# Channel attention and gated convolution: where the weight conversions and the norm sums of the first score pass run

## Chip, cores and metric

The kernel runs on one NeuronCore of a Trainium2 chip. The metric is the device time of one execution in microseconds (us); lower is better. A core has these engines, each with an instruction queue of its own that it works off in order: TensorE (PE, matmuls; PEld is its weight load), VectorE (DVE), ScalarE (ACT), GpSimd (POOL) and SyncE (SP), which here only issues DMAs. Operands lie in SBUF, 128 partitions wide, and matmul results in PSUM.

## The reference, cut to what matters

```
# q, k, v: (4, 6336, 256) float32; conv_w: (5, 256); w_val, w_out: (256, 256)
qn = q / (norm(q, axis=1) + 1e-6)            # norms over the 6336 rows, per channel
kn = k / (norm(k, axis=1) + 1e-6)
a  = softmax(kn^T @ qn / tau, axis=-1)       # 256 x 256 per batch
x  = v @ a
gate_pre[t] = sum over tap 0..4 of conv_w[tap] * x[t - 4 + tap]
out = (sigmoid(gate_pre) * (x @ w_val)) @ w_out
```

The three weights arrive as float64 and the rest as float32, so the kernel sees each weight as pairs of 32-bit integers and makes the float32 (or its high and low part) out of these itself.

## The kernel before, in words

**Two kinds of work.** For each of the four batches a *score pass* goes over all rows of q and k and gathers s = k^T q in one PSUM tile (`s_ps`) and the sums of the squares of q and k in two tiles (`acc`, named `acc_ps`, in PSUM, and `side`, named `acc`, in SBUF). A softmax makes the 256 x 256 weights from them. Then a *step* for each of 13 chunks of 508 rows takes v through two products, the five-tap gate, the sigmoid and the product with w_out. From the second batch on, the score pass of the next batch is mixed with the steps of this one. The first batch's score pass stands alone, at the head of the program: that is where the change is.

**The score pass in groups.** A batch's rows are cut into 17 groups. Group 0 holds one row per partition and a rest of 64 rows, groups 1 to 16 three rows per partition each. `load_group` fetches the q and the k of a group with two DMAs from the SP queue into one of six `raw` buffers, four groups ahead. `score_group` (L166) then puts out, per group:

- ScalarE: the squares `sq` of the group (L209), into one of two buffers. For a row that is *split*, also the high part `hi` (L192).
- VectorE: rows j < `nv` of `sq` are added to the sum in PSUM (L214).
- GpSimd: the other rows are added to the sum in SBUF (L214, too), and the low part of a split row is raw minus hi (L193).
- TensorE (L226): rows j < `nw` are multiplied as they are (*native*: two matmuls a row, which the trace records as four), the others as three products of their high and low parts (six matmuls a row).

In the first batch groups 0 to 10 have nw = 3 and nv = 2: all native, VectorE adds two rows and GpSimd one. Groups 11 to 16 have nw = 2 and nv = 3: two native rows and one split row, VectorE adds all three, GpSimd only makes the low part.

**What waits for what.** A group's squares need a free `sq` buffer, that is, the adds of an earlier group on both engines. The squares must be made before the `raw` buffer is loaded again. After group 16 the softmax begins: VectorE joins the sums into `acc_all` (L240), which waits for every add, ScalarE copies s out of PSUM (L242), and TensorE clears `s_ps` for the second batch (L231) behind that copy, does the second batch's group 0 and then sums `acc_all` over the partitions (L245). Five groups of the second batch, all native, fill TensorE while the softmax runs.

**The weights.** At group 6 the kernel asks for the weights. `prepare_weights(0)` (w_val and conv_w, into `wa`) is ten VectorE instructions and a reciprocal (L161), `prepare_weights(1)` (w_out, into `wb`, `wo_hi` and `wo_lo`) nine and a ScalarE copy, `wo_hi` (L149). L132, L136, L138, L140 and L144 read one tensor each; L134, L142, L146, L151 and L154 read two. All of these lie in SBUF. Both parts are generators, and from group 9 on each takes two instructions a group, so the two are mixed. A scheduler with a model of the times then sets the final order on each engine; `issue_after` and `behind(...)` hold it back.

## Time and profile before

| | |
|---|---|
| Median of 3 runs | 657.69 us (655.65 to 657.83) |
| The profiled execution | 655.7 us, of which 653.8 us are the span from the first to the last instruction |
| TensorE busy | 636.1 us, 97% of the span |
| VectorE, ScalarE, GpSimd busy | 521.7 us (80%), 465.7 us (71%), 362.1 us (55%) |

The profile's timeline gives, per engine, the start of an instruction in us from the span's start, how long it took, its line, its operation, what it writes and reads, how many alike were run together (x), and in brackets the idle time of the engine ahead of it with what ended it. An instruction that is held up inside the engine shows as a longer one. The chain of waits is followed back from the program's last instruction to what released each step.

### The profile page before, as it was taken

How to read it: one execution, taken by the hardware profiler on the slowest of the kernel's cores; microseconds unless marked ns; L12 is line 12 of the kernel's file. 1: busy time of each engine (PE TensorE's matmuls, PEld its weight loads, DVE VectorE, ACT ScalarE, POOL GpSimd, SP SyncE). 2: the span in 40 equal slices, each digit the busy share in tenths (PEclk: the TensorE clock that was granted, in tenths of full speed). 3: DMA queues.
4: the chain of work that ended last, by engine and by line, in shares of the span. 5: the costliest groups of instructions: out<-in, count | busy, mean ns of one | idle time of the engine just before them, and what ended most of it. 6: DMA issues, size and time to landing. Idle time of an engine off the chain costs nothing.

```text
span 653.8 us, 10657 instructions
## 1 busy us (share of the span) xinstructions
PE 636.1 (97%) x4008; PEld 570.3 (87%) x4008; DVE 521.7 (80%) x831; ACT 465.7 (71%) x607; POOL 362.1 (55%) x174
## 2 busy tenths in 40 slices
PE   7999999999999999999998999999999999999996
PEld 5878799998979999999997998999999798988886
DVE  3897689787878688778788688778778889888894
ACT  5465978867888768668688787777777755655564
POOL 2441896965837769659565497766763122312221
PEclk9999999999999999999999999999999999999999
DMA  8999875555635665545554375653222343443213
GB/s 272 336 320 335 267 233 154 152 170 162 188 99 175 186 195 176 167 136 173 177 178 127 113 222 168 179 182 103 65 80 76 113 126 102 114 129 105 65 51 99
DMA packets 107875, 105.75 MB, mean 162 GB/s; under 512 B 5744, under 2 KB 107312, under 8 KB 107824
## 3 DMA queue, kind: packets, MB, share of 16 engines
q1 hardware_dynamic: 82048, 79.76, 39.8%
q10 hardware_dynamic: 25776, 25.32, 13.7%
q8 instruction: 31, 0.51, 0.3%
q14 instruction: 20, 0.16, 0.1%
HBM read 79.11 MB, written 25.95 MB: 161 GB/s over the span
## 4 chain that ended last, share of the span: by engine, by line
PE 84%; DVE 4%; ACT 4%; DMA 3%; SPq 2%; POOL 1%; issue 1%; ACTq 0%; DVEq 0%
PE o_ps L404 21%; PE x_ps L345 19%; PE val_ps L345 19%; PE s_ps L226 17%; PE t_ps L335 6%; SPq L74 2%; DMA raw<-in_k_dram 1%; PE o_ps L294 1%; POOL hi L193 1%; DMA w_raw<-in_moe_conv_w_dram 1%; DMA v_raw<-in_v_dram 1%; ACT hi L192 1%; DVE acc_ps L214 1%; DVE gate L361 1%; DVE gate L374 1%
## 5 line engine op out<-in xcount | busy, mean ns | idle before, releaser
L361 DVE SCALAR_TENSOR_TENSOR gate<-x_ps,wa,gate 128x508 f32<-128x508 f32 (+1 forms) x416 | 275.4, 718 | 14.4 <-ACT gate L359 13.4
L193 POOL TENSOR_TENSOR hi<-raw,hi 128x1536 fp32r<-128x1536 f32 (+2 forms) x54 | 167.8, 3109 | 92.8 <-ACT hi L192 92.8
L388 POOL TENSOR_TENSOR g_lo<-gate,g_hi 128x1016 fp32r<-128x1016 f32 (+1 forms) x50 | 116.8, 2335 | 145.1 <-ACT g_hi L387 130.5
L214 DVE TENSOR_TENSOR acc_ps<-acc_ps,sq 128x512 f32<-128x512 f32 (+1 forms) x134 | 93.5, 698 | 73.9 <-ACT sq L209 70.7
L345 PE MATMUL x_ps<-v_hi,w 128*128 128x512 f32 (+1 forms) x416 | 138.1, 391 | 0.0
L345 PE MATMUL val_ps<-v_hi,w 128*128 128x508 f32 (+1 forms) x416 | 133.9, 384 | 0.8 <-ACT o_sb L414 0.7
L226 PE MATMUL s_ps<-hi 128*128 128x256 f32 (+1 forms) x852 | 121.0, 287 | 6.2 <-ACT hi L192 4.0
L226 PEld LDWEIGHTS s_ps<-hi 128*128 128x128 f32 (+1 forms) x852 | 110.7, 190 | 12.6 <-ACT hi L192 5.5
L404 PE MATMUL o_ps<-wo_hi,g_hi 128*128 128x256 f32 x400 | 113.3, 283 | 0.2 <-DVE gate L374 0.2
L414 ACT COPY o_sb<-o_ps 128x512 f32<-128x512 f32 x99 | 58.1, 588 | 76.1 <-PE o_ps L404 74.8
L404 PE MATMUL o_ps<-wo_lo,g_hi 128*128 128x256 f32 x400 | 112.2, 281 | 0.0
L404 PE MATMUL o_ps<-wo_hi,g_lo 128*128 128x256 f32 x400 | 111.8, 280 | 0.0
L209 ACT ACTIVATE sq<-raw 128x1536 f32<-128x1536 f32 (+3 forms) x69 | 96.0, 1393 | 16.3 <-DVE acc_ps L214 8.0
L214 POOL TENSOR_TENSOR acc<-acc,sq 128x512 f32<-128x512 f32 x58 | 76.3, 1315 | 38.9 <-ACT sq L209 38.5
L345 PEld LDWEIGHTS val_ps<-v_hi,w 128*128 128x128 f32 x416 | 77.2, 188 | 14.4 <-ACT o_sb L414 0.9
L345 PEld LDWEIGHTS x_ps<-v_hi,w 128*128 128x128 f32 x416 | 77.5, 188 | 13.9 <-DVE gate L361 0.2
L359 ACT ACTIVATE gate<-x_ps,wa 128x508 f32<-128x508 f32 (+1 forms) x104 | 68.1, 669 | 20.6 <-PE x_ps L345 20.3
L336 ACT CAST v_hi<-t_ps 128x512 fp32r<-128x512 f32 (+1 forms) x104 | 55.7, 568 | 35.7 <-PE t_ps L335 33.2
L345 PE MATMUL x_ps<-v_lo,w 128*128 128x512 f32 (+1 forms) x208 | 79.8, 384 | 0.0
L345 PE MATMUL val_ps<-v_lo,w 128*128 128x508 f32 (+1 forms) x208 | 79.3, 381 | 0.0
L374 DVE TENSOR_TENSOR gate<-val_ps,gate 128x508 f32<-128x508 f32 (+1 forms) x104 | 64.3, 657 | 17.1 <-ACT gate L367 14.4
L404 PEld LDWEIGHTS o_ps<-wo_hi,g_hi 128*128 128x128 f32 x400 | 75.3, 188 | 1.4 <-DVE gate L374 0.4
(84 smaller groups left out, 800.0 us busy)
## 6 DMA issues: line engine op xcount, KB each, us to landing
raw<-in_q_dram SPq DMA_DIRECT2D x64, 384.0 KB
raw<-in_k_dram SPq DMA_DIRECT2D x64, 384.0 KB
v_raw<-in_v_dram SPq DMA_DIRECT2D x44, 512.0 KB
out_dram<-o_sb ACTq DMA_DIRECT2D x47, 384.0 KB
out_dram<-o_sb ACTq DMA_DIRECT2D x47, 124.0 KB
v_raw<-in_v_dram SPq DMA_DIRECT2D x4, 384.0 KB
raw<-in_q_dram SPq DMA_DIRECT2D x4, 128.0 KB
raw<-in_k_dram SPq DMA_DIRECT2D x4, 128.0 KB
```

The lines of the kernel that those rows point to most:

```text
L193: nc.gpsimd.tensor_tensor(hi[r, js, :, 1, :], raw[r, js, :, :], hi[r, js, :, 0, :].bitcast(F32), ALU.subtract)
L209: nc.scalar.activation(sq[0:np_, ja:jb], raw[0:np_, ja:jb], AF.Square)
L214: eng.tensor_tensor(st[key][0:np_], st[key][0:np_], sq[0:np_, j], ALU.add)
L226: nc.tensor.matmul(st["s"][:, h, :], lhs, rhs, start=False, stop=stop and h == NH - 1 and n_ == len(ops) - 1)
L336: nc.scalar.copy(th[:, h, 0:w], tp[:, 0:w])
L345: marks["PRODUCT"] = nc.tensor.matmul(ps, wt[:, which, ws, ch, hs], vs[:, ch, lo:hi_], start=n_ == 0, stop=n_ == 3 * NH - 1)
L359: nc.scalar.activation(gate[:, h, 0:w], x_ps[:, 0:w], AF.Copy, scale=cw[:, h, 0:1])
L361: nc.vector.scalar_tensor_tensor(gate[:, h, 0:w], x_ps[:, tap:tap + w], cw[:, h, tap:tap + 1], gate[:, h, 0:w], ALU.mult, ALU.add)
L374: nc.vector.tensor_tensor(gate[:, h, 0:w], val_ps[:, 0:w], gate[:, h, 0:w], ALU.mult)
L388: nc.gpsimd.tensor_tensor(gl[:, :, 0:w], gate[:, :, 0:w], gh[:, :, 0:w].bitcast(F32), ALU.subtract)
L404: nc.tensor.matmul(o_ps[:, u * C:(u + 1) * C], gs[:, h, off:off + P], ws[:, h, :], start=n_ == 0, stop=n_ == 3 * NH - 1)
L414: marks["ACT"] = nc.scalar.copy(o_sb[:, j:j + len(pair), :], o_ps[:, 0:len(pair) * C].rearrange("p (j c) -> p j c", c=C))
```

## The change

Three things change in the first score pass and behind the first softmax:

- Groups 7 to 13 (`SIDE` = 7 to `MIXED` = 14) are all native, and VectorE adds only one of their three rows, GpSimd two. Before, groups 7 to 10 were native with one row for GpSimd, and 11 to 13 had a split row and no row for GpSimd. Groups 14 to 16 stay as they were.
- From group 7 on, three conversion instructions a group are put out, held behind the last VectorE add of that group, first all of `prepare_weights(0)`, then all of `prepare_weights(1)`.
- The ScalarE copy `wo_hi` leaves the generator and stands behind the first softmax, behind its last ScalarE instruction (L298).

```diff
-SIDE = 11
+SIDE, MIXED = 7, 14
...
-            if part:
-                nc.scalar.copy(wo_hi.rearrange("p h e -> p (h e)"), up.bitcast(F32))
...
-            nw, nv = (GROUP, 2) if g < SIDE else (2, 3)
+            nw, nv = (GROUP, 2 if g < SIDE else 1) if g < MIXED else (2, 3)
...
-            eng.tensor_tensor(st[key][0:np_], st[key][0:np_], sq[0:np_, j], ALU.add)
+            add = eng.tensor_tensor(st[key][0:np_], st[key][0:np_], sq[0:np_, j], ALU.add)
+            if key == "acc":
+                marks["DVE"] = add
...
-        if n >= 9:
-            for gen in prep:
-                for _ in range(2):
-                    next(gen, 0)
+        if n >= SIDE:
+
+            with behind("DVE"):
+                for _ in range(3):
+                    while prep and next(prep[0], 0) is not None:
+                        prep.pop(0)
...
     while stages:
         tick()
+    if WORDS == 2:
+        with behind("ACT"):
+            nc.scalar.copy(wo_hi.rearrange("p h e -> p (h e)"), w_raw[1][:, :, 1].bitcast(F32))
     for h in range(NH):
         transpose_v(*step(1), h)
```

In the changed kernel the lines of `prepare_weights` and `score_group` behind the removed two stand two lower: the adds are L212, the casts L190, the low parts L191, the last conversion of w_out L149.

**VectorE, the last conversions of w_out (`wb`, `w_raw_206`) and the end of the score pass.** Before, `sq_271` holds the squares of group 10, and `sq_290`, `sq_315`, `sq_356`, `sq_378`, `sq_397`, `sq_418` those of groups 11 to 16:

```order
L144 TENSOR_SCALAR w_raw_206<-w_raw_206 128x512
L151 SCALAR_TENSOR_TENSOR wo_lo_112<-w_raw_206,wb_110 128x512
L214 TENSOR_TENSOR acc_ps_120<-acc_ps_120,sq_271 128x512
L146 TENSOR_TENSOR w_raw_206<-w_raw_206,wb_110 128x512
L214 TENSOR_TENSOR acc_ps_120<-acc_ps_120,sq_271 128x512
L214 TENSOR_TENSOR acc_ps_120<-acc_ps_120,sq_290 128x512 x3
L214 TENSOR_TENSOR acc_ps_120<-acc_ps_120,sq_315 128x512 x3
L214 TENSOR_TENSOR acc_ps_120<-acc_ps_120,sq_356 128x512 x3
L214 TENSOR_TENSOR acc_ps_120<-acc_ps_120,sq_378 128x512 x3
```

Changed, `sq_294`, `sq_311`, `sq_344`, `sq_357`, `sq_375`, `sq_396` are groups 11 to 16:

```order
L212 TENSOR_TENSOR acc_ps_120<-acc_ps_120,sq_311 128x512
L142 SCALAR_TENSOR_TENSOR wb_110<-w_raw_206,wb_110 128x512
L144 TENSOR_SCALAR w_raw_206<-w_raw_206 128x512
L146 TENSOR_TENSOR w_raw_206<-w_raw_206,wb_110 128x512
L212 TENSOR_TENSOR acc_ps_120<-acc_ps_120,sq_344 128x512
L149 SCALAR_TENSOR_TENSOR wo_lo_112<-w_raw_206,wb_110 128x512
L212 TENSOR_TENSOR acc_ps_120<-acc_ps_120,sq_357 128x512 x3
L212 TENSOR_TENSOR acc_ps_120<-acc_ps_120,sq_375 128x512 x3
L212 TENSOR_TENSOR acc_ps_120<-acc_ps_120,sq_396 128x512 x3
L240 TENSOR_TENSOR acc_all_428<-acc_ps_120,acc_121 128x512
```

The last conversion stood between the adds of group 10, with 19 adds still to come; now it stands behind the add of group 13, with the nine adds of groups 14 to 16 to come. The first conversion (L132 of `wa`) now stands behind the add of group 7; before it stood between the two adds of group 6.

**GpSimd in the same stretch.** Before, from group 7 (`sq_225`) to group 16:

```order
L214 TENSOR_TENSOR acc_121<-acc_121,sq_225 128x512
L214 TENSOR_TENSOR acc_121<-acc_121,sq_239 128x512
L214 TENSOR_TENSOR acc_121<-acc_121,sq_253 128x512
L214 TENSOR_TENSOR acc_121<-acc_121,sq_271 128x512
L193 TENSOR_TENSOR hi_289<-raw_222,hi_289 128x2x256
L193 TENSOR_TENSOR hi_314<-raw_236,hi_314 128x2x256
L193 TENSOR_TENSOR hi_355<-raw_250,hi_355 128x2x256
L193 TENSOR_TENSOR hi_377<-raw_268,hi_377 128x2x256
L193 TENSOR_TENSOR hi_396<-raw_286,hi_396 128x2x256
L193 TENSOR_TENSOR hi_417<-raw_311,hi_417 128x2x256
```

Changed, again from group 7 (`sq_225`) to group 16 (`hi_395`):

```order
L212 TENSOR_TENSOR acc_121<-acc_121,sq_225 128x512 x2
L212 TENSOR_TENSOR acc_121<-acc_121,sq_242 128x512 x2
L212 TENSOR_TENSOR acc_121<-acc_121,sq_259 128x512 x2
L212 TENSOR_TENSOR acc_121<-acc_121,sq_276 128x512 x2
L212 TENSOR_TENSOR acc_121<-acc_121,sq_294 128x512 x2
L212 TENSOR_TENSOR acc_121<-acc_121,sq_311 128x512 x2
L191 TENSOR_TENSOR hi_356<-raw_273,hi_356 128x2x256
L212 TENSOR_TENSOR acc_121<-acc_121,sq_344 128x512
L191 TENSOR_TENSOR hi_374<-raw_291,hi_374 128x2x256
L212 TENSOR_TENSOR acc_121<-acc_121,sq_344 128x512
L191 TENSOR_TENSOR hi_395<-raw_308,hi_395 128x2x256
```

Ten instructions have become seventeen: four adds and six low parts before, fourteen adds and three low parts now, and all of the conversions stand beside them on VectorE.

**ScalarE behind the first softmax.** Before, the softmax's last cast (L298) is followed by the high part of the second batch's group 5 (`hi_611`):

```order
L289 COPY at_583<-o_ps_525 128x512
L359 ACTIVATE gate_558<-x_ps_559,wa_109 128x508
L359 ACTIVATE gate_558<-x_ps_571,wa_109 128x508
L298 CAST w_522<-o_ps_585 128x512
L192 CAST hi_611<-raw_460 128x6x256
L209 ACTIVATE sq_612<-raw_460 128x1536
```

Changed (that group's high part is `hi_590`):

```order
L289 COPY at_561<-o_ps_503 128x512
L359 ACTIVATE gate_536<-x_ps_537,wa_109 128x508
L359 ACTIVATE gate_536<-x_ps_549,wa_109 128x508
L298 CAST w_500<-o_ps_563 128x512
L525 CAST wo_hi_111<-w_raw_206 128x512
L190 CAST hi_590<-raw_438 128x6x256
L207 ACTIVATE sq_591<-raw_438 128x1536
```

The copy of w_out's high part, which stood between the squares of group 11 and the high part of group 12, now stands in front of that cast.

## Prediction

> **What bounds the kernel now.** I read the page first, then the chain of waits, then the timeline of each engine over the first 90 us, where the change is. The page:
>
> ```profile
> span 653.8 us, 10657 instructions
> PE 636.1 (97%) x4008; PEld 570.3 (87%) x4008; DVE 521.7 (80%) x831; ACT 465.7 (71%) x607; POOL 362.1 (55%) x174
> ```
>
> TensorE is busy for 97% of the span, so a change counts only where TensorE idles, or where it makes TensorE idle. TensorE's timeline of the first score pass and the start of the second:
>
> ```profile
> 4.25 34.65 PE L226 MATMUL s_ps<-raw 128*128 128x256 f32 x136 [1.85 <-DMA raw<-in_k_dram]
> 42.17 0.38 PE L226 MATMUL s_ps<-hi 128*128 128x256 f32 x1 [0.38 <-ACT hi L192]
> 43.54 0.86 PE L226 MATMUL s_ps<-hi 128*128 128x256 f32 x5 [0.98 <-POOL hi L193]
> 44.23 1.89 PE L226 MATMUL s_ps<-raw 128*128 128x256 f32 x8
> 46.67 1.89 PE L226 MATMUL s_ps<-raw 128*128 128x256 f32 x8
> 53.09 1.06 PE L226 MATMUL s_ps<-hi 128*128 128x256 f32 x6
> 54.83 0.50 PE L231 MATMUL s_ps<-zeros 128*128 128x512 f32 x1 [0.67 <-DMA v_raw<-in_v_dram]
> 57.18 0.70 PE L245 MATMUL o_ps<-acc_all,ones 128*128 128x256 f32 x2
> ```
>
> From 4.25 on it works without a gap through groups 0 to 10 and the two native rows of group 11. Then it waits for the high part (0.38 us at 42.17) and the low part (0.98 us at 43.54) of group 12. From 44.23 mixed groups follow each other every 2.44 us (46.67 - 44.23), and the pass ends at 54.15 (53.09 + 1.06). What held group 12 up is on ScalarE:
>
> ```profile
> 40.95 0.66 ACT L149 CAST wo_hi<-w_raw 128x512 fp32r<-128x512 f32 x1 [2.47 <-DVE w_raw L146]
> 52.96 0.63 ACT L209 ACTIVATE sq<-raw 64x512 f32<-64x512 f32 x1 [0.77 <-DVE acc_ps L214]
> 54.19 0.58 ACT L242 COPY s<-s_ps 128x512 f32<-128x512 f32 x1 [0.59 <-PE s_ps L226]
> ```
>
> The copy `wo_hi` stands idle for 2.47 us until VectorE has made its input, and the high part of group 12 is queued behind it. The other two rows are the end of the pass: the squares of the second batch's rest rows (52.96), which wait for VectorE's adds, then the copy of s (54.19), behind which TensorE clears `s_ps` (54.83) and, 2.35 us on, sums `acc_all` (57.18), which begins the softmax.
>
> Data is no bound there: the last k of the first batch is on the way from 38.96 to 47.78, in the chain of waits:
>
> ```profile
> 38.96 8.82 DMA raw<-in_k_dram
> ```
>
> **What the change removes.** The wait of ScalarE goes, and groups 11 to 13 need no high and low part. TensorE alone would then be the bound. A native group is a third of the 36 native matmuls at 61.62 (7.94 us, of which some 0.2 are the last one's tail), 2.59 us:
>
> ```profile
> 61.62 7.94 PE L226 MATMUL s_ps<-raw 128*128 128x256 f32 x36
> ```
>
> From 38.53 there are four records of group 11 (0.86), two native groups (5.18) and three mixed ones (7.32): 51.9, and with the last matmul's tail 52.1, against 54.15. That is the most the change can bring here: 2.0 us.
>
> **What it adds: a conflict of VectorE and GpSimd.** VectorE's rows while the conversions run, and GpSimd's in the same stretch:
>
> ```profile
> 25.39 0.70 DVE L142 SCALAR_TENSOR_TENSOR wa<-w_raw,wa 128x522 int32<-128x522 int32 x1
> 26.01 1.49 DVE L132 TENSOR_SCALAR wb<-w_raw 128x512 int32<-128x512 int32 x1
> 28.02 0.42 DVE L144 TENSOR_SCALAR w_raw<-w_raw 128x522 int32<-128x522 int32 x1
> 29.56 1.62 DVE L146 TENSOR_TENSOR w_raw<-w_raw,wa 128x522 int32<-128x522 int32 x1
> 32.05 0.68 DVE L214 TENSOR_TENSOR acc_ps<-acc_ps,sq 128x512 f32<-128x512 f32 x1
> 36.81 1.23 DVE L144 TENSOR_SCALAR w_raw<-w_raw 128x512 int32<-128x512 int32 x1
> 37.95 1.76 DVE L151 SCALAR_TENSOR_TENSOR wo_lo<-w_raw,wb 128x512 fp32r<-128x512 int32 x1
> ```
>
> ```profile
> 25.64 1.58 POOL L214 TENSOR_TENSOR acc<-acc,sq 128x512 f32<-128x512 f32 x1 [3.19 <-ACT sq L209]
> 29.33 1.27 POOL L214 TENSOR_TENSOR acc<-acc,sq 128x512 f32<-128x512 f32 x1 [2.12 <-ACT sq L209]
> 31.54 1.72 POOL L214 TENSOR_TENSOR acc<-acc,sq 128x512 f32<-128x512 f32 x1 [0.94 <-ACT sq L209]
> 36.47 1.28 POOL L214 TENSOR_TENSOR acc<-acc,sq 128x512 f32<-128x512 f32 x1 [3.21 <-ACT sq L209]
> 37.70 1.46 POOL L193 TENSOR_TENSOR hi<-raw,hi 128x512 fp32r<-128x512 f32 x1
> ```
>
> L144 takes 0.42 us at 28.02, where GpSimd is idle, but 1.23 at 36.81, and it ends at 38.04, 0.29 us behind the GpSimd add that ended at 37.75. L132 at 26.01 takes 1.49 and ends 0.28 behind the one that ended at 27.22. The conversions that read two tensors take 0.70 alone (25.39); met by GpSimd they take 1.62 and 1.76 and end 0.58 and 0.55 behind its instruction (30.60 and 39.16). It works the other way, too: a GpSimd add of 1.27 (29.33) takes 1.58 where L142 is ahead of it and ends 1.13 behind that (27.22 - 26.09), and the low part at 37.70 ends 1.12 behind L144. So whole instructions exclude each other, and they take turns: L144 comes in between GpSimd's two instructions, and GpSimd's second one ahead of L151. An add into PSUM is not held: 0.68 at 32.05, in the midst of GpSimd's 31.54 to 33.26.
>
> [...]
>
> Before, ten GpSimd instructions stood between group 7 and the pass's end, and five of them met conversions. Changed, the order has seventeen, fourteen adds and three low parts, all beside the conversions. Behind a held conversion stands the next group's add, and behind that add ScalarE's squares of a later group. No DMA is moved there. Taking turns costs 17 x 1.13 = 19.2 us for GpSimd, 10 x 0.29 = 2.9 us for the one-tensor conversions and 9 x 0.56 = 5.0 us for the two-tensor ones: 27.1 us in a row. It begins when group 7's squares are there:
>
> ```profile
> 24.01 1.48 ACT L209 ACTIVATE sq<-raw 128x1536 f32<-128x1536 f32 x1 [2.97 <-DVE w_raw L134]
> ```
>
> 24.01 + 1.48 = 25.49, GpSimd at 25.64, as now. 25.64 + 27.1 = 52.7; going through the order instruction by instruction with these prices, I get 53.0 for the end of the last conversion (GpSimd is idle for about a microsecond before group 8's squares, and some conversions run free while it waits for group 14's high part). Before it ended at 40.91 (40.24 + 0.67):
>
> ```profile
> 40.24 0.67 DVE L146 TENSOR_TENSOR w_raw<-w_raw,wb 128x512 int32<-128x512 int32 x1
> 40.84 9.77 DVE L214 TENSOR_TENSOR acc_ps<-acc_ps,sq 128x512 f32<-128x512 f32 x13
> 55.25 0.69 DVE L240 TENSOR_TENSOR acc_all<-acc_ps,acc 128x512 f32<-128x512 f32 x1
> ```
>
> Before, the nineteen adds to come then ran in 13 x 0.75 and six more, and `acc_all` ended at 55.94. Changed, nine adds of 0.73 to 0.75 stand behind 53.0, and by its waits ScalarE's squares of group 15 take the buffer of group 14. So: three adds to 55.2, squares of group 15 to 56.7, three adds to 58.95, the rest rows' squares (0.63 at 52.96 above) and the copy of s (0.58, overlapping by 0.1) to 60.1. Group 16's adds and `acc_all` end at 61.8. TensorE, through with group 16 at about 55 by the same steps, clears `s_ps` at 60.1 instead of 54.83: **+5.3 us**. The sum over `acc_all` stays 2.35 us behind that (62.5; `acc_all` is there by 61.8), so the whole softmax and the five groups that fill it move by 5.3.
>
> Going through before in the same way gives `acc_all` at 55.1 where the trace has 55.94, so the method is, if anything, short by 0.8.
>
> **The copy of w_out's high part.** It now stands in front of the cast at 75.23, on a path without slack:
>
> ```profile
> 74.75 0.59 ACT L298 CAST w<-o_ps 128x512 fp32r<-128x512 f32 x1 [0.92 <-PE o_ps L294]
> 75.23 1.48 ACT L192 CAST hi<-raw 128x1536 fp32r<-128x1536 f32 x1
> ```
>
> ```profile
> 76.78 3.51 POOL L193 TENSOR_TENSOR hi<-raw,hi 128x1536 fp32r<-128x1536 f32 x1 [0.65 <-ACT hi L192]
> ```
>
> ```profile
> 80.35 2.42 PE L226 MATMUL s_ps<-hi 128*128 128x256 f32 x18 [0.51 <-POOL hi L193]
> ```
>
> ScalarE's cast starts as soon as L298 is through, GpSimd's low part follows it, and TensorE idles 0.51 us for that at 80.35. The copy takes 0.66 (40.95 above), less the 0.1 by which ScalarE's instructions overlap: **+0.56 us**. A gain is excluded, since ScalarE was waiting for nothing else there; nothing is the low end, if TensorE's two products of the first step come later than the low part.
>
> **Behind that.** TensorE's longest idle time in the middle of the program is 2.69 us:
>
> ```profile
> 356.91 0.39 PE L226 MATMUL s_ps<-hi 128*128 128x256 f32 x1 [2.69 <-ACT hi L192]
> ```
>
> It waits for ScalarE's cast there, which moves along with everything ahead of it, so it gives nothing back. TensorE's order changes in a few places from there on; no work is added, and I take 0, with 1 us either way.
>
> **Sum.** 5.3 + 0.56 = 5.9 us: the profiled execution would take 655.7 + 5.9 = 661.6. It is 2.0 under the median of the runs, so for the median I give 657.69 + 5.9 = **663.6 us**.
>
> **Rivals.**
>
> *The conflict doesn't bind (not slower).* If the two engines fall into each other's gaps, or VectorE gets through its conversions while GpSimd waits, the pass is bound by TensorE: -2.0 + 0.56 = -1.4, or 656.2 us. For it: the meetings above cost VectorE only 0.8 to 1.1 us each, and TensorE ran on through all of them up to 38.5. Against it: GpSimd has two adds a group, 2.5 us of a native group's 2.59, so there are no gaps. It decides where the last conversion ends: 7.1 us lie between that and the clear, and the sum is nought if TensorE clears at 54.3, so by 47.2, which needs 5.8 of the 27.1 us to vanish.
>
> *The conflict costs half.* If an engine now and then gets two instructions in a row, or conversions run free in more of GpSimd's waits, the last one ends at about 49.5: +1.8 + 0.56, or 660.0 us.
>
> *TensorE slows down after its idle time.* Changed, it idles from 55 to 60. TensorE's matmuls of the pass (L226) in two stretches: the stretch, its length, TensorE's busy time with its records, the weight loads', the granted clock, the DMA share and GB/s:
>
> ```profile
> 8.00:12.00 4.00, 4.00 (x10) 3.06 (x10) 1.00 1.07 348
> 20.00:24.00 4.00, 4.00 (x20) 3.54 (x19) 1.00 1.10 311
> ```
>
> The kernel starts at half the pace, 10 records in 4 us and later 20, though the clock column has 1.00 for both. If five idle microseconds bring that back, the eight records ahead of the sum over `acc_all` take twice their 1.9 us: 663.6 + 1.9 = 665.5 us. Against it: after the 2.69 us of idle time above, the next product's twelve matmuls (357.30, in the chain of waits) take no longer than others:
>
> ```profile
> 357.30 2.75 PE x_ps L345 x12
> 382.29 2.74 PE x_ps L345 x12
> ```
>
> [...]
>
> **How the numbers follow.** The forecast has 0.52: conflict and turns are in the rows, only how far they add up is worked out. The slower TensorE has 0.18, half the cost 0.16, no cost 0.14. The forecast's own range is 661.5 to 665.5. The range goes down to 656.0, where the first rival stands, and up to 667.0: the slower TensorE with the method's 0.8 and some reordering. About 0.5%, or 3.3 us, is what a measurement of this kernel can tell from no change, so slower begins at 661.0 and faster below 654.4. Slower: 0.93 x 0.52 + 0.18 + 0.1 x 0.16 = 0.68. Faster: 0.05, from the no-cost rival with a lucky reordering. The same: 0.27.
>
> **What would show it.** Right: conversions of 0.9 to 1.8 us between 26 and 53, GpSimd busy throughout that stretch, `acc_all` ending near 62, L231 near 60 with about 5 us of idle TensorE ahead of it, and TensorE's wait ahead of the first `hi` matmuls of the second batch about 1 us. The forecast is wrong if the last conversion ends before 47, or if L231 starts before 56. A first product of the second batch at 0.4 us a matmul shows the slower TensorE.

## The result, and the profile after

The changed kernel takes 668.95 us in the median of four executions (667.69, 667.94, 669.95 and 1282.15); the last one was disturbed, and without it, as in the ratio below, the median is 667.94. The kernel before takes 657.26 (four executions, 655.65 to 657.83). The ratio is 1.017, with a 95% interval of 1.0151 to 1.0189. The forecast was slower, 663.6 us, with a range up to 667.0: the direction came, and the time lies above the range by either median.

The page of the changed kernel: the span, the busy time, and the granted clock in 40 slices.

```profile
span 668.2 us, 10625 instructions
...
PE 642.5 (96%) x4002; PEld 573.5 (86%) x4002; DVE 524.2 (78%) x821; ACT 464.8 (70%) x604; POOL 373.2 (56%) x181
...
PEclk9997899999999999999999899999999999999999
```

TensorE is busy for 6.4 us more than before, although it has no work more. The last row says why: in slices 4 and 5 (50 to 84 us) and again in slice 23 the clock is below full speed. The trace of before has no such slice. This is TensorE's timeline (start, length, line, what it writes and reads, records, idle time ahead):

```profile
47.97 0.38 PE L226 MATMUL s_ps<-hi 128*128 128x256 f32 x1 [0.85 <-ACT hi L190]
...
55.77 0.85 PE L226 MATMUL s_ps<-hi 128*128 128x256 f32 x5 [0.66 <-POOL hi L191]
61.67 0.80 PE L231 MATMUL s_ps<-zeros 128*128 128x512 f32 x1 [5.05 <-ACT s L242]
62.27 3.91 PE L226 MATMUL s_ps<-raw 128*128 128x256 f32 x8
...
67.83 5.13 PE L226 MATMUL s_ps<-raw 128*128 128x256 f32 x12
...
73.68 7.94 PE L226 MATMUL s_ps<-raw 128*128 128x256 f32 x36
```

The pass ends at 56.62 and the clear (L231) follows at 61.67, behind 5.05 us of idle time. What comes next is the part that the forecast priced too low: eight records take 3.91 us, and it is full pace again at the 36 native matmuls, 7.94 us as before. In the kernel before, the eight records behind the clear take 2.08 us:

```profile
55.16 2.08 PE L226 MATMUL s_ps<-raw 128*128 128x256 f32 x8
```

From the clear to these 36 it is 73.68 - 61.67 = 12.01 us; before it was 61.62 - 54.83 = 6.79. That is 5.2 us.

VectorE's timeline, a conversion in the midst of the pass, the last one, and what stands behind it:

```profile
33.95 1.65 DVE L142 SCALAR_TENSOR_TENSOR wa<-w_raw,wa 128x522 int32<-128x522 int32 x1
...
53.42 1.16 DVE L149 SCALAR_TENSOR_TENSOR wo_lo<-w_raw,wb 128x512 fp32r<-128x512 int32 x1
54.51 2.15 DVE L212 TENSOR_TENSOR acc_ps<-acc_ps,sq 128x512 f32<-128x512 f32 x3
58.27 4.44 DVE L212 TENSOR_TENSOR acc_ps<-acc_ps,sq 128x512 f32<-128x512 f32 x6 [1.61 <-ACT sq L207]
62.82 0.69 DVE L240 TENSOR_TENSOR acc_all<-acc_ps,acc 128x512 f32<-128x512 f32 x1
```

GpSimd's timeline beside it, ten adds in a row and a later low part:

```profile
30.94 15.42 POOL L212 TENSOR_TENSOR acc<-acc,sq 128x512 f32<-128x512 f32 x10 [1.21 <-ACT sq L207]
...
54.00 1.72 POOL L191 TENSOR_TENSOR hi<-raw,hi 128x512 fp32r<-128x512 f32 x1
```

The add takes 15.42 / 10 = 1.54 us here, and a conversion that took 0.70 alone takes 1.65. The last conversion ends at 54.58, and ScalarE shows how the squares of the last two groups wait for VectorE:

```profile
25.43 1.48 ACT L207 ACTIVATE sq<-raw 128x1536 f32<-128x1536 f32 x1 [2.70 <-DMA raw<-in_k_dram]
...
56.76 2.86 ACT L207 ACTIVATE sq<-raw 128x1536 f32<-128x1536 f32 x2 [5.97 <-DVE acc_ps L212]
...
61.06 0.56 ACT L242 COPY s<-s_ps 128x512 f32<-128x512 f32 x1
...
87.04 0.67 ACT L525 CAST wo_hi<-w_raw 128x512 fp32r<-128x512 f32 x1
```

The first of these rows tells something else: in this execution group 7's squares start at 25.43, where they started at 24.01 before, since the data came 1.42 us later. That is scatter: in the experiments below they start anywhere between 24.05 and 26.14, and at 24.08 in a kernel whose program is the changed one's up to there (one GpSimd add a group). The delay is passed on: with work in the idle time, below, the squares start 0.62 us later still, and the last conversion and the clear come 0.46 us later.

Now the granted clock, asked for in stretches whose borders are those of the clock's own changes (stretch, its length, TensorE's busy time with its records, the granted clock, the DMA share, GB/s):

```profile
55.43:58.84 3.41, 0.85 (x5) 1.00 1.09 354
58.84:62.26 3.42, 0.59 (x1) 0.50 1.05 332
62.26:65.67 3.41, 3.41 (x9) 0.50 0.85 267
65.67:69.08 3.41, 3.41 (x11) 0.50 0.46 138
69.08:72.50 3.42, 3.42 (x9) 0.50 0.27 95
72.50:75.91 3.41, 3.41 (x21) 1.00 0.51 138
366.04:369.45 3.41, 0.72 (x6) 1.00 0.40 140
369.45:372.87 3.42, 3.42 (x9) 0.50 0.36 87
```

A stretch of 3.41 us in which TensorE was busy for only 0.85 us is followed by half the clock, and in the head that lasts for four stretches, 13.7 us, of which 10.8 have work. At 366 it happens once more, behind the 2.69 us of idle time that cost nothing in the profiled execution of the kernel before. There the next product takes 4.28 us in the chain of waits, and not 2.75:

```profile
369.26 0.44 PE s_ps L226
369.70 4.28 PE x_ps L345 x12
```

The mean granted clock of this execution is 0.986, and 0.985 and 0.986 in the two others of the three: they were at half pace for about as long.

So the span is 668.2 - 653.8 = 14.4 us longer: about 1.4 later data, 5.4 the later clear (61.67 - 54.83 - 1.42), 5.2 the half pace behind it, 0.3 the copy of w_out's high part (the second batch's hi matmuls start 12.36 us later than before, at 92.71, where the 36 native ones were 12.06 later), 1.5 the half pace at 369, and 0.6 that I have not placed.

### The profile page after: what moved, and what is told of

Read it like the earlier page. It is cut to its first block, busy times and chain, and to the rows that moved or that the text cites. A ratio compares the mean times of both kernels' runs of the same rounds, so it can differ in the third digit from the quotient of the medians.

```text
span 668.2 us, 10625 instructions
## 1 busy us (share of the span) xinstructions
PE 642.5 (96%) x4002; PEld 573.5 (86%) x4002; DVE 524.2 (78%) x821; ACT 464.8 (70%) x604; POOL 373.2 (56%) x181
## 4 chain that ended last, share of the span: by engine, by line
PE 83%; DVE 6%; ACT 5%; DMA 3%; issue 1%; POOL 1%; SPq 1%; ACTq 0%
PE o_ps L404 20%; PE x_ps L345 19%; PE val_ps L345 19%; PE s_ps L226 17%; PE t_ps L335 6%; DMA raw<-in_k_dram 2%; ACT sq L207 2%; DVE acc_ps L212 2%; POOL hi L191 1%; DVE gate L361 1%; PE o_ps L294 1%; ACT hi L190 1%; DMA v_raw<-in_v_dram 1%; DVE w_raw L146 0%; DVE gate L374 0%
## 5 line engine op out<-in xcount | busy, mean ns | idle before, releaser
L191 POOL TENSOR_TENSOR hi<-raw,hi 128x1536 fp32r<-128x1536 f32 (+2 forms) x51 | 164.3, 3223 | 87.9 <-ACT hi L190 87.9
L212 DVE TENSOR_TENSOR acc_ps<-acc_ps,sq 128x512 f32<-128x512 f32 (+1 forms) x124 | 86.5, 697 | 79.2 <-ACT sq L207 76.3
L226 PE MATMUL s_ps<-hi 128*128 128x256 f32 x834 | 118.0, 286 | 7.4 <-ACT hi L190 3.9
L226 PEld LDWEIGHTS s_ps<-hi 128*128 128x128 f32 x834 | 107.9, 190 | 13.5 <-POOL hi L191 5.1
L212 POOL TENSOR_TENSOR acc<-acc,sq 128x512 f32<-128x512 f32 x68 | 91.2, 1342 | 43.3 <-ACT sq L207 42.1
L374 DVE TENSOR_TENSOR gate<-val_ps,gate 128x508 f32<-128x508 f32 (+1 forms) x104 | 64.3, 657 | 17.2 <-ACT gate L367 14.4
L337 DVE TENSOR_TENSOR v_lo<-t_ps,v_hi 128x512 fp32r<-128x512 f32 (+1 forms) x104 | 66.2, 659 | 13.6 <-ACT v_hi L336 13.6
```

What stands on the lines that cost most here:

```text
L191: nc.gpsimd.tensor_tensor(hi[r, js, :, 1, :], raw[r, js, :, :], hi[r, js, :, 0, :].bitcast(F32), ALU.subtract)
L212: add = eng.tensor_tensor(st[key][0:np_], st[key][0:np_], sq[0:np_, j], ALU.add)
L226: nc.tensor.matmul(st["s"][:, h, :], lhs, rhs, start=False, stop=stop and h == NH - 1 and n_ == len(ops) - 1)
L337: nc.vector.tensor_tensor(tl[:, h, 0:w], tp[:, 0:w], th[:, h, 0:w].bitcast(F32), ALU.subtract)
L374: nc.vector.tensor_tensor(gate[:, h, 0:w], val_ps[:, 0:w], gate[:, h, 0:w], ALU.mult)
```

## Experiments

Two theories stood against each other once the trace was read. The first: the conflict of VectorE and GpSimd moves the clear by 5.4 us, and the idle time that it leaves TensorE brings half pace, which costs about as much again. The rivals: the conversions' later place or GpSimd's many adds do it without a conflict; and the slow matmuls come from something else than the idle time.

### Without the conversions

The conversions are left out of the changed kernel. `wa` and `wo_lo` are constants that VectorE writes at the start, and `wo_hi` is copied from words that nothing has converted; so the output isn't the reference's.

```diff
+    nc.vector.memset(wa, 0.01)
+    nc.vector.memset(wo_lo.bitcast(F32), 0.0)
...
-            nc.vector.tensor_scalar(f, up, 0x1FF, 15, ALU.bitwise_and, ALU.logical_shift_left)
...
-                nc.vector.tensor_tensor(w, w, up.bitcast(F32), ALU.add)
```

> The changed kernel without the weight conversions: VectorE sets the float32 weights to constants at the program's start, the rest is as in the changed kernel, so the output is not the reference's. Theory (whole instructions of VectorE and GpSimd exclude each other, and that holds the squares and the end of the pass up): with no conversion to meet, GpSimd's fourteen adds run at 1.27 us each beside VectorE's adds; the pass ends near 53, acc_all near 54, L231 starts at 52 to 55 with under 2 us of idle TensorE, TensorE keeps its pace, and the time is 654 to 657 us. Rival (GpSimd's two adds a group, 2.5 us of 2.6, are too slow by themselves): L231 stays near 58 to 62 and the time is 662 us or more.

Measured: 656.5 us, ratio 0.9984 (0.9975 to 0.9993). GpSimd's ten adds and the clear (here L211):

```profile
31.31 13.45 POOL L192 TENSOR_TENSOR acc<-acc,sq 128x512 f32<-128x512 f32 x10 [1.11 <-ACT sq L187]
```

```profile
54.15 0.50 PE L211 MATMUL s_ps<-zeros 128*128 128x512 f32 x1 [1.36 <-ACT s L222]
54.49 2.08 PE L206 MATMUL s_ps<-raw 128*128 128x256 f32 x8
```

The same 17 GpSimd instructions without conversions beside them take 1.35 us an add (1.27 was expected), not 1.54, the clear comes at 54.15, and the eight records behind it take 2.08 us, the full pace. So GpSimd's adds alone harm nothing; it is the meeting. It also shows the ceiling of the whole idea: with the conversions free of charge, the clear comes 0.68 us sooner than before and the kernel gains 0.16%.

### One GpSimd add a group

In groups 7 to 13 of the changed kernel GpSimd adds one of its two rows; the squares of the other rows are left out of the sum.

```diff
-            if j in where:
+            if j in where or (b == 0 and SIDE <= g < MIXED and j == 1):
```

> The changed kernel with the conversions where it has them, but GpSimd adds only one of its two rows in groups 7 to 13 (the other row's squares are left out of the norms, so the output is not the reference's). Theory: ten GpSimd instructions instead of seventeen meet the conversions, 7 x 1.1 = 7.9 us less; the last conversion ends at 45 to 48, L231 starts at 53 to 56, and the time is 655 to 659 us. Rival (the conversions' later place in VectorE's queue does it, whatever GpSimd has to do): the last conversion still ends at 52 to 55 and the time stays at 666 to 670 us.

Measured: 661.93 us, ratio 1.0068 (1.0047 to 1.009). VectorE, then TensorE:

```profile
45.89 1.16 DVE L149 SCALAR_TENSOR_TENSOR wo_lo<-w_raw,wb 128x512 fp32r<-128x512 int32 x1
46.98 6.70 DVE L212 TENSOR_TENSOR acc_ps<-acc_ps,sq 128x512 f32<-128x512 f32 x9
```

```profile
54.52 1.22 PE L245 MATMUL o_ps<-acc_all,ones 128*128 128x256 f32 x2 [2.65 <-DVE acc_all L240]
```

Seven GpSimd instructions fewer, and with the conversions in the same place of the program the last one ends at 47.05 and not 54.58; 1.35 of these 7.5 us are earlier data (group 7's squares start at 24.08). With the run before this settles the conflict: without either side of it the delay is gone. The time, though, missed its expectation: TensorE's order came out differently, it sums `acc_all` ahead of the clear and idles 2.65 us for it, and that sufficed for two stretches at half pace (54.04 to 60.87).

### Idle time by itself, and the same with work in it

In the kernel before, seven GpSimd adds on a spare tile run at the end of the first pass, and a matmul of one column that waits for them stands ahead of the clear. The second kernel has the same and seven matmuls of 512 columns, whose result nobody reads, while TensorE waits.

```diff
...
+    pad = soft_p.tile([P, 512], F32, name="pad")
+    with behind("POOL"):
+        nc.gpsimd.tensor_tensor(pad, zeros.bitcast(F32), zeros.bitcast(F32), ALU.add)
+        for _ in range(6):
+            nc.gpsimd.tensor_tensor(pad, pad, zeros.bitcast(F32), ALU.add)
+    idle = ps.tile([P, 512], F32, name="idle_ps", tag="bank")
+    marks["IDLE"] = nc.tensor.matmul(idle[:, 0:1], ident, pad[:, 0:1], start=True, stop=True)
...
```

```diff
...
+    fill = ps.tile([P, 512], F32, name="fill_ps", tag="bank")
+    with behind("SCORE"):
+        for n in range(7):
+            marks["FILL"] = nc.tensor.matmul(fill, ident, wa[:, 0:512], start=True, stop=True)
...
```

> The kernel before, with seven GpSimd adds on a spare tile behind the last low part of the first pass, and a one-column matmul that waits for them between TensorE's last matmul of the pass and L231: TensorE idles some 7 us there (54.2 to about 61) and nothing else is done to it. Theory (TensorE falls to half its pace after an idle stretch, and that is the part of the result that the forecast left out): L231 starts 6.5 us later than before, the following matmuls take 0.43 us a record for some 10 us, and the time is 657.3 + 6.5 + 4 to 5.5 = 668 to 669 us. Rival (idle time costs only itself): 663.8 us.

> As the one with seven GpSimd adds, but TensorE does seven matmuls of 512 columns on a spare PSUM tile (about 6 us) while it waits. Theory: the same start of L231, about 61, but TensorE keeps its pace, 0.22 us a record from L231 on: 657.3 + 6.5 = 663.8 us, 4 to 5.5 us less than without the matmuls. Rival (the pace behind L231 has another cause than the idle time): the two take the same time.

Measured: 668.17 us (ratio 1.0158, 1.0143 to 1.0173) with idle time, 663.86 (1.0091, 1.0076 to 1.0106) with work in it. TensorE's timelines, idle first:

```profile
60.93 0.58 PE L506 MATMUL idle_ps<-pad,ident 128*128 128x1 f32 x2 [6.75 <-POOL pad L504]
61.38 0.77 PE L231 MATMUL s_ps<-zeros 128*128 128x512 f32 x1
61.95 3.91 PE L226 MATMUL s_ps<-raw 128*128 128x256 f32 x8
```

```profile
54.33 6.17 PE L509 MATMUL fill_ps<-wa,ident 128*128 128x512 f32 x14
61.25 0.38 PE L510 MATMUL idle_ps<-pad,ident 128*128 128x1 f32 x2 [0.75 <-POOL pad L504]
61.49 0.48 PE L231 MATMUL s_ps<-zeros 128*128 128x512 f32 x1
61.81 2.08 PE L226 MATMUL s_ps<-raw 128*128 128x256 f32 x8
```

The clear stands within 0.11 us in both, the eight records take 3.91 and 2.08 us, and the medians differ by 4.3 us. TensorE's idleness alone, with none of the change, costs that. That it is a lack of work and not the wait is shown by matmuls that compute nothing useful.

### The changed kernel with work in its idle time

```diff
...
+    fill = ps.tile([P, 512], F32, name="fill_ps", tag="bank")
+    with behind("SCORE"):
+        for n in range(5):
+            nc.tensor.matmul(fill, ident, wa[:, 0:512], start=True, stop=True)
     run_group()
```

> The changed kernel with five matmuls of 512 columns (identity by the value weights, onto a spare PSUM tile that nobody reads) behind the last score matmul of the first batch and ahead of the clear of s_ps (L231), so TensorE works through most of its 5 us of idle time; VectorE, GpSimd and ScalarE have the same instructions as in the changed kernel. Theory (the changed kernel's 11.5 us are the conflict's 5.4 us, which moves the clear, and about 5 us more because TensorE runs at half its pace behind that idle time): the clear stays within 1.0 us of where the changed kernel has it, the eight records behind it take about 2 us and not 3.9, from the clear to the 36 native matmuls it is 6.8 us and not 12.0, and the time falls by 4 to 6 us to 663 to 665 (ratio 1.008 to 1.012). Rival one (the slow matmuls there come from something else that the change does, a busier memory or the reordering): the rows stay at half pace and the time stays at 667.5 to 670. Rival two (TensorE's idle time isn't what decides, any low activity of the whole pass does): the same as rival one.

Measured: 665.2 us (662.22 to 665.89), ratio 1.0123 (1.0085 to 1.016). TensorE's timeline, then two stretches of the pass ahead of it:

```profile
62.13 0.50 PE L231 MATMUL s_ps<-zeros 128*128 128x512 f32 x1 [0.66 <-ACT s L242]
62.47 2.08 PE L226 MATMUL s_ps<-raw 128*128 128x256 f32 x8
...
68.93 7.94 PE L226 MATMUL s_ps<-raw 128*128 128x256 f32 x36
```

```profile
46.96:50.37 3.41, 1.64 (x9) 1.00 0.93 228
50.37:53.79 3.42, 3.42 (x12) 0.50 0.99 321
```

From the clear to the 36 matmuls it is 6.80 us, as in the kernel before. The 5.2 us are gone, and the clear has stayed. The time is a little above what was expected (663 to 665 us), and the second fence shows a cost that was not on the list: the two waits of group 14 (0.81 and 0.96 us) fell into one stretch here, TensorE was busy for 1.64 of 3.41 us, and the next stretch ran at half pace. In the changed kernel's execution a border at 48.60 (three stretches of 3.41 us ahead of the clock's change at 58.84) cut the same waits (0.85 and 0.97 us) in two, TensorE was busy for 2.33 and 2.69 us of the two stretches, and the clock stayed at 1.00.

### The parts alone

First the copy of w_out's high part behind the softmax, in the kernel before:

```diff
-            if part:
-                nc.scalar.copy(wo_hi.rearrange("p h e -> p (h e)"), up.bitcast(F32))
...
+    if WORDS == 2:
+        with behind("ACT"):
+            nc.scalar.copy(wo_hi.rearrange("p h e -> p (h e)"), w_raw[1][:, :, 1].bitcast(F32))
```

> The kernel before with one part of the change alone: the copy of w_out's high part taken from its place among the conversions to behind the first softmax. The prediction's step (+0.56 us on ScalarE's path to the second batch's first low part, and group 12's high part no longer waits): 42.17 loses its wait of 0.38 us and 43.54 some of its 0.98, the pass ends 0.4 to 1.4 us sooner if GpSimd's low parts allow it, and the second batch's first hi matmuls wait 0.5 to 0.6 us longer: 656.5 to 658.2, no difference that can be measured (ratio 0.998 to 1.001). Rival (the copy costs more at its new place, since the cast behind it then collides with others): over 659.5. Rival (the 1.4 us of waits in the first pass come back in full): 656.2 or less.

Then the conversions in turn from group 7, with the groups as before:

```diff
-SIDE = 11
+SIDE, MIXED = 7, 14
...
-            nw, nv = (GROUP, 2) if g < SIDE else (2, 3)
+            nw, nv = (GROUP, 2) if g < 11 else (2, 3)
...
-        if n >= 9:
-            for gen in prep:
-                for _ in range(2):
-                    next(gen, 0)
+        if n >= SIDE:
+            with behind("DVE"):
+                for _ in range(3):
+                    while prep and next(prep[0], 0) is not None:
+                        prep.pop(0)
```

> The kernel before with the second part of the change alone: the conversions, three a group from group 7 on, in turn behind VectorE's adds; groups 11 to 13 stay mixed, VectorE adds two rows of the groups up to 10 and all three behind, GpSimd one row a group, and the copy of w_out's high part stays in the conversions' course. Theory (the harm is the number of GpSimd's whole instructions that meet the conversions): GpSimd has 10 instructions there as before and not 17; the last conversion ends at 45 to 49 (VectorE has about six adds more ahead of it than before), the clear (L231) comes at 53.5 to 56, TensorE never idles over 2.5 us, no half pace; 655.5 to 659.5 (ratio 0.997 to 1.003). Rival (the later place of the conversions is the harm in itself): the last conversion ends behind 51, the clear behind 58, and the time is 663 or more.

And the groups alone, with the conversions and the copy as before:

```diff
-SIDE = 11
+SIDE, MIXED = 7, 14
...
-            nw, nv = (GROUP, 2) if g < SIDE else (2, 3)
+            nw, nv = (GROUP, 2 if g < SIDE else 1) if g < MIXED else (2, 3)
```

> The kernel before with the first part of the change alone: groups 11 to 13 native, and GpSimd adds two of three rows in groups 7 to 13, with the conversions where they were before (two generators by two steps from group 9's turn) and the copy of w_out's high part in its old place, which the program's order now puts in front of the squares of groups 11 to 13. Theory (17 GpSimd instructions beside the conversions are the harm wherever the conversions stand): thirteen conversions are still to come when the two adds a group begin, at about 1.55 us each with GpSimd's turns, so the last ends at about 46 instead of 41; the copy then holds the squares of groups 11 to 13 and the high part of group 14 to 51 to 53; TensorE idles 4 to 6 us in front of group 14's high matmuls, the clear comes at 59 to 62, and half pace follows; 664 to 670 (ratio 1.010 to 1.018). Rival (it is the turns between conversions and adds, not the number of GpSimd's adds, that hurt): the last conversion ends before 43 and the time stays at 655.5 to 659.5.

**The copy alone**: 657.75 us, ratio 1.0013 (0.9998 to 1.0028), no difference, as expected. TensorE's wait for the second batch's first low part:

```profile
81.22 2.42 PE L224 MATMUL s_ps<-hi 128*128 128x256 f32 x18 [0.96 <-POOL hi L191]
```

It starts 0.87 us later than before, of which the pass had brought 0.29 (the 36 native matmuls start at 61.91, not 61.62): 0.58, where the forecast's step had 0.56. In the first pass the waits only changed place (0.80 and 0.97 us), and it ends at 54.21.

**The turns alone**: 659.85 us, ratio 1.0046 (1.0025 to 1.0068). VectorE, and TensorE's clear (here L233):

```profile
50.90 1.16 DVE L151 SCALAR_TENSOR_TENSOR wo_lo<-w_raw,wb 128x512 fp32r<-128x512 int32 x1
```

```profile
56.23 0.50 PE L233 MATMUL s_ps<-zeros 128*128 128x512 f32 x1 [1.37 <-ACT s L244]
```

The last conversion ends at 52.06 and not at 45 to 49, which was the rival's sign (behind 51). The clear, at 56.23, comes 0.2 us above the theory's range and short of the rival's 58, and the time is a little above the theory's range. So the later place does cost something even with ten GpSimd instructions, 2.35 us at the 36 native matmuls (63.97), but far less than 12.06, and there is no half pace in the head (the eight records behind the clear take 2.08 us, the 36 native ones 7.94). How far the place alone would move the clear isn't shown: VectorE has 17 adds for groups 7 to 13 here and seven in the changed kernel, and ScalarE copies s ahead of the rest rows' squares here (55.62 and 56.49), but behind them in the changed kernel (61.06 and 60.52). That GpSimd's instructions make the delay rests on the run with one add a group, which leaves out nothing but GpSimd instructions.

**The groups alone**: 662.06 us, ratio 1.0085 (1.0059 to 1.0111). ScalarE, then TensorE:

```profile
42.61 0.67 ACT L149 CAST wo_hi<-w_raw 128x512 fp32r<-128x512 f32 x1 [4.30 <-DVE w_raw L146]
```

```profile
49.50 0.38 PE L226 MATMUL s_ps<-hi 128*128 128x256 f32 x1 [2.25 <-ACT hi L192]
51.40 1.44 PE L226 MATMUL s_ps<-hi 128*128 128x256 f32 x5 [1.52 <-POOL hi L193]
...
60.54 0.51 PE L231 MATMUL s_ps<-zeros 128*128 128x512 f32 x1 [0.68 <-ACT s L242]
```

Here the theory's step on the conversions failed: the last one ends at 42.57, not 46, since GpSimd waits for squares three times in between (1.01, 1.19 and 3.38 us). The third wait is the copy's doing: it waits 4.30 us for VectorE, and the squares of groups 11 to 13 stand behind it. The clear at 60.54 is in the range given, though part of that may be scatter (group 7's squares start at 26.14 here, 2.13 us later than before); the time lies below the theory's range and above the rival's. The 3.8 us of idle time in front of group 14 brought half pace for two stretches (50.4 to 57.2). All later rows are 5.7 us behind those of before. So neither part is harmless alone, and each harms in another way.

### Work in, or another order around, the idle time at 354 us

The traces so far show the clock changing on a grid of 3.41 us (last section), which lies elsewhere from one execution to another (TensorE's pace first changes at 13.88 us in the kernel before and at 11.06 in the changed one), so that, by my estimate, the 2.69 us at 354 of the kernel before cost half a stretch in some executions, as at 369 above (1.5 us), and nothing in others. Two versions of the kernel before go at that place: the first fills it, the second takes the waiting matmul out of the way.

```diff
...
+        if n == 23:
+            fill = ps.tile([P, 512], F32, name="fill_ps", tag="bank")
+            with behind("O"):
+                for _ in range(2):
+                    marks["FILL"] = nc.tensor.matmul(fill, ident, wa[:, 0:512], start=True, stop=True)
...
-                run_group()
+                with behind(*["FILL"] if n == 23 else []):
+                    run_group()
```

```diff
...
-                run_group()
+                with behind(*["CONV"] if n == 23 else []):
+                    run_group()
```

> The kernel before with two matmuls of 512 columns (identity by the value weights, onto a spare PSUM tile that nobody reads) in TensorE's idle time of 2.69 us at 354, behind the output projection and ahead of the one hi matmul that waits there for ScalarE's cast; nothing else is moved. Theory (in the runs so far every stretch of a grid of 3.413 us in which TensorE was busy for 0.48 or less was followed by half pace in the next stretch, and none in which it was busy for 0.50 or more; where the grid lies is settled at each start, so the 2.69 us cost 1.6 us in some executions and nothing in others): the two take 1.8 of the 2.69 us, no stretch there falls under 0.50, the clock is never halved between 15 and 640 us, and all executions lie within 0.3% of each other at 654.9 to 656.2, against a median of 656.5 to 657.7 of the kernel before in the same call (ratio 0.997 to 0.999). Rival (the 1.6 us come and go for another reason, or the extra work only costs): the ratio is 1.000 or above, and the scatter is that of before.

> The kernel before with one matmul moved: the single hi matmul of a score group that waits 2.69 us at 354 for ScalarE's cast goes behind the twelve matmuls of the next gate product, which stood behind it on TensorE's queue. Nothing is added and nothing left out. Theory: the first gate product can start when VectorE's fourth tap has freed its buffer, at about 354.2, the second when the other buffer is free, at about 357.4 and not 358.5, so TensorE gains about 1.0 us there, and its idle time falls in two pieces of which none brings half pace; ScalarE and VectorE follow: 654 to 656 in nearly all executions (ratio 0.995 to 0.998). Rival (the cast's readers behind it, or ScalarE's exponentials, hold the same work anyway): the time saved there is waited out again within 20 us, and the ratio is 0.999 to 1.002.

**Filled**: 656.12 us (twelve executions, 655.72 to 657.30), ratio 0.9975 (0.9962 to 0.9988), the fastest version here and the only one that beats the kernel before by more than 0.2%. Ratio and spread are as expected, though five of the twelve lie above the 656.2 that was given. The kernel before, measured beside it, scattered from 655.81 to 660.22 in 23 executions. Two useless matmuls make the kernel faster in the median and its times narrower. That it is the clock that they change is borne out twice. The profiled execution here and that of the kernel before, neither with half pace in its middle, have the same span, 653.8 us. And of all 52 executions of the kernel before that stand beside the experiments, the 17 with a mean granted clock of 0.999 have a median of 656.1 us, the 35 with a lower one 657.9. The stretch with the matmuls in it:

```profile
353.51:356.93 3.42, 2.58 (x12) 1.00 0.40 138
```

**Moved**: 657.26 us, ratio 0.9993 (0.9977 to 1.0009), no difference; the expectation failed. The gate product that was to start at 354.2 waits itself:

```profile
356.89 0.77 PE L345 MATMUL x_ps<-v_hi,w 128*128 128x512 f32 x1 [2.64 <-ACT hi L192]
```

It starts when ScalarE's cast ends (355.41 + 1.48), as the matmul did that stood ahead of it before. So the idle time stays in one piece, and in this execution half pace follows it (356.50 to 359.91: single matmuls of 0.63 us, and of 0.39 to 0.40 from 359.98 on). What of that cast the product needs, the trace doesn't say; it stays open.

## Why the direction was right and the size wrong

- **What bounds the kernel, and what the change removes.** Right. TensorE could have ended the pass some 2 us sooner; the changed kernel without conversions comes to 52.8, where the forecast had 52.1 as the bound. That data is no bound was not quite so: TensorE waits 0.67 and 0.75 us for k there. Without the conversions the kernel gains 0.16%.
- **The conflict of VectorE and GpSimd.** Right in kind and size. Going through the order from 25.64 on gave 53.0 for the last conversion (the plain sum of 27.1 us gave 52.7); the stretch ran from 27.06 to 54.58, and with the later data taken off that is 53.2. That the turns go on through seventeen instructions was an estimate from the rows of two; in the trace ten adds in a row take 1.54 us each. The clear was forecast 5.3 us later and is 5.4 later. The steps behind it (three adds, squares of group 15, three adds, the rest rows, the copy of s) stand in the trace in that order.
- **The copy of w_out's high part.** Right: 0.58 us by itself and 0.30 in the changed kernel, where 0.56 was forecast.
- **Later reorderings, 0 with 1 us either way.** Wrong by 1.5 us in the profiled execution. No reordering did it, but the half pace at 369, which depends on where the grid lies.
- **TensorE behind its idle time.** This is the step that failed. The forecast's sum, 5.3 + 0.56, puts TensorE's own pace at nothing. The prediction has it as a rival only, by which the eight records ahead of the sum over `acc_all` "take twice their 1.9 us" (2.08 in the trace), with a chance of 0.18 and a price of 1.9 us; that half pace would last for these eight records alone was an estimate that no run had shown. It came, and it cost 5.2 us, since half pace lasted not for eight records but for all of TensorE's work from 61.67 to 72.50. With five matmuls in the idle time these 5.2 us are gone, and 6.75 us of idle time put into the kernel before cost 4.3 us more than the same wait with work in it. With 5.2 in place of 1.9, the rival's own sum is 668.8 us; 668.95 was measured, or 667.94 in the median of the three. That it comes so close is partly luck, since the sum has neither the half pace at 369 nor the scatter of the data.
- **Why it was held unlikely.** The evidence against it was that 2.69 us of idle time left the next product at 2.75 us. That was one execution, and one draw of the grid. In it a border at 355.21, 100 stretches of 3.413 us behind the first change of pace at 13.88, cut the idle time in two:

```profile
351.80:355.21 3.41, 2.43 (x21) 1.00 0.45 154
355.21:358.62 3.41, 1.71 (x8) 1.00 0.46 124
```

In the changed kernel the same 2.69 us fell into one stretch, the one from 366.04 to 369.45, with 0.72 us of work. The start of the program had shown the state and how long it lasted there. In the kernel before it works at half pace from 4.25 to 13.88, for 9.6 us (9 records in the last 3.41 us of that, 17 in the next 3.41). Half pace of that length costs 4.8 us and not 1.9; it deserved more weight.
- **The sign to look for.** The prediction named "a first product of the second batch at 0.4 us a matmul". That product stands at 81.81, behind the end of half pace, and single matmuls of it take 0.39 to 0.48 us in both kernels. The sign was in the rows right behind the clear.

## What to carry to other kernels

Price an idle time of the bounding engine twice: for itself, and for the slow stretch that may follow, which here cost as much as the wait (5.2 us behind 5.05). Before moving work from one engine to another, look whether the two can run side by side at all; an engine with free time is no help if each of its instructions shuts the other out, as here (1.65 us for a conversion of 0.70). And a wait that one execution shows to be harmless isn't shown to be harmless if its cost depends on a phase that differs from execution to execution, as here (2.69 us of idle time left the next product at 2.75 us in one trace and at 4.28 in another): look at several executions, and at the scatter.

## What the hardware showed that I had not expected

**The clock follows a grid and a share.** In the changed kernel's trace TensorE's pace first changes at 11.06 us (9 records in the 3.41 us ahead of that, 17 in the next 3.41), and the granted clock changes at 58.84, 72.50, 369.45 and 372.87; from each of these five to the next it is 14, 4, 87 and 1 stretches of 3.413 us. In that of the kernel before the pace first changes at 13.88, and the clock at 652.17, 187 such stretches later. In the experiments half pace lasted for one of them (50.37 to 53.79, the changed kernel with five matmuls), two (54.04 to 60.87, one GpSimd add a group) or four (56.76 to 70.41, seven spare adds). The grid's place varies between executions (11.06 and 13.88). Six stretches at full pace in which TensorE was busy for at most 0.48 of the time were each followed by half pace: 0.85 and 0.72 us of 3.41 in the changed kernel, 0.69 with the groups alone, 0.83 with the seven spare adds, 1.26 with one add a group, 1.64 with the five matmuls. In the traces of the two kernels the ten stretches between 15 and 640 us with a share of 0.50 to 0.79 (1.71 to 2.70 us of 3.41) were not. The closest pair is 1.64 of 3.41 us (slow afterwards) and 1.71 of 3.41 (not): a half-idle stretch was enough.

**The way back can be long.** Behind one stretch with little work half pace lasted for one stretch (369.45 to 372.87 here) or two (54.04 to 60.87 in the kernel with one add a group); behind two in a row it lasted for three more, though TensorE had work in them (62.26 to 72.50 here, 60.17 to 70.41 in the kernel with seven spare adds). At the start of the program, too, half pace lasted long, for 9.6 us of work in the kernel before. Why it takes three is open: the kinds of matmul in these stretches differ too (one-column ones and 64-row ones among them), and no run separates the two.

**VectorE and GpSimd.** Whole instructions shut each other out in these traces: with both queues full, an add of GpSimd took 1.54 us, and 1.35 without conversions beside it, and a conversion that took 0.70 alone took 1.65. Adds into PSUM were free of it here, too (0.69 at 35.52 in the changed kernel, between two held conversions).
